# Scores of an attention kernel computed one period earlier, a transpose moved to another PSUM bank, reciprocals moved up in VectorE's order

## Chip, cores and metric

One Trainium2 chip, one of its cores. The metric is the device time of one execution in microseconds (us); lower is better. The engines are TensorE (PE, with its weight loads as PEld), VectorE (DVE), ScalarE (ACT), GpSimd (POOL), and SyncE (SP), which issues the loads and stores here.

## What is computed

Attention that keeps the 32 largest scores of each query, and behind it four chained matrix products on all tokens. Cut to what matters:

```python
B, H, S, D = 8, 8, 576, 64
scores = (1 / 8) * q @ k.T                    # per batch and head, 576 x 576
kth = the 32nd largest score of each row
scores = where(scores >= kth, scores, -1e9)
attn = exp(scores - max) / (sum + 1e-9)
x = (attn @ v) with the heads side by side    # 4608 tokens x 512
out = (((x @ w1) * (x @ w2)) @ w3) @ w_out
```

Inputs and output are float32.

## The kernel before

**Slots and periods.** The queries of a batch are cut into four tiles of 128 and one of 64. A slot is one such tile for one pair of heads (the tiles of 64 take two pairs), so there are 18 slots per batch and 144 in all. A slot has 128 x 2 rows of scores of 576 columns each, in planes `a` = 0 and 1. The loop `for p in range(-1, n_slots + 4)` (line 523) is one period per pass; in it five slots are at different steps: in period `p`, slot `i = p + 1` gets its scores, slot `p` its 32 largest, slot `j = p - 1` its mask and exponentials, slot `l = p - 2` its normalisation, and slot `m = p - 3` its transposition and value products. `InOrder` (line 49) keeps each engine's instructions in the order in which the program records them, so the order of the lines in the loop is the order on each engine, and each engine waits at an instruction until that one may run.

**One period, engine by engine.**
- TensorE: some products of the chained matrices (`fill`), the transposition `turn` (line 291), more `fill`, `scores` (line 201), the value products `values` (line 309), more `fill`. Value products of two slots are put together in every second period (`put_back`), so the time repeats in pairs of periods. Each pair has 48 products of `fill`.
- VectorE: the fold of slot `p`, four operations on two tensors that spread the three thirds of each row into maxima and minima (`w`, in `top32_steps`, line 226); after a period with value products the low halves of `x` (`split_low`); then three rounds of MAX8 and MATCH_REPLACE8 and a last MAX8 on the whole row. Between the rounds it takes the reciprocals of the sums (`invert`) and the product `asb` for the chained matrices.
- ScalarE: two relus that begin the mask (`mask`), the copy of the transposes `tp` back over `pab` and of the odd chunk `pr` (`take_turned`, line 302), two normalisations, the exponentials of plane 0, the copy of the first half of the scores (`take_scores`), the exponentials of plane 1, the second copy of scores, and casts and copies for `x`, `g`, `asb`, `osb`.
- POOL: 1e-9 onto the sums (`add_up`), the thresholds `edge` and the check values `over` from the 32 largest, two masks `pab<-s,pab` of 128 x 576, which are tied behind the fold, and the low halves `g<-asb,g`.

**PSUM.** Eight banks: two buffers of two banks for scores and transposes (`ps_a`; `st` and `tp` take turns in them), one bank `vo`, three for the chained products. A score tile uses columns 0 to 287 of each of its two banks. The transposition of a slot is nine blocks of 128 x 128; eight of them fill `tp`, and the ninth, the odd chunk (columns 512 to 639 of the flat row), is written to `vo[:, :128]`. The value products lie in `vo[:, 256:512]`, where ScalarE (`split_high`) and VectorE (`split_low`) read them.

**The three stretches.** In the first 13 periods the weights are unpacked (`warm`, `decode`), then come the periods with `fill`, and at the end the last block of chained products without attention.

Of the kernel before, what the change touches and what calls it, by code (L numbers as in the profile page):

```python
# [9 lines left out]
F32 = mybir.dt.float32  # L10
# [59 lines left out]
def attn_moe(ctx: ExitStack, tc: tile.TileContext, q, k, v, w1, w2, w3, w_out, out, flag, any_missed, general):  # L70
# [148 lines left out]
    def new_s():  # L219
        return att_p.tile([128, 2, S], F32, tag="s", name="s", bufs=S_BUFS)  # L220

    def take_scores(s, st, h):
        lo, hi = HALVES[h]
        act.copy(s[:, :, lo:hi], st[h][:, :, :HS])

    def top32_steps(s, slot):
        w = att_p.tile([128, 2, S], F32, tag="w", name="w", bufs=1)
        top = tops[slot % len(tops)]
        one, two, three = slice(0, NG), slice(NG, 2 * NG), slice(2 * NG, S)
        dve.tensor_tensor(w[:, :, three], s[:, :, one], s[:, :, two], op=ALU.max)  # L230
        dve.tensor_tensor(w[:, :, two], s[:, :, one], s[:, :, two], op=ALU.min)
        dve.tensor_tensor(w[:, :, one], w[:, :, three], s[:, :, three], op=ALU.max)
        yield dve.tensor_tensor(w[:, :, three], w[:, :, three], s[:, :, three], op=ALU.min)
        for i in range(4):
            cut = slice(i * 8, (i + 1) * 8)
            for a in range(2):
                dve.max(top[:, a, cut], w[:, a, one] if i < 3 else w[:, a, :])
            if i < 3:
                for a in range(2):
                    dve.match_replace(w[:, a, one], top[:, a, cut], w[:, a, one], NEG)  # L240
                yield
# [40 lines left out]
    def invert(sums):  # L282
        dve.reciprocal(sums, sums)
# [4 lines left out]

    vo = ps_v.tile([128, 512], F32, name="vo")

    def turn(pab):
        tp = ps_a.tile([128, 2, 512], F32, tag="a", name="tp")
        flat = pab[:].rearrange("p a c -> p (a c)")
        for a in range(2):
            for c in range(4):
                o = a * (S + 64) + c * 128
                pe.transpose(tp[:, a, c * 128 : (c + 1) * 128], flat[:, o : o + 128], ident)
            if a == 0:
                pe.transpose(vo[:, :128], flat[:, 512:640], ident)
        return tp  # L300

    def take_turned(pab, tp):
        pts = pab[:].rearrange("p a c -> p (a c)")[:, :1024].rearrange("p (a c) -> p a c", a=2)
        act.copy(pts, tp)
        pr = att_p.tile([128, 128], F32, tag="pr", name="pr")
        act.copy(pr, vo[:, :128])
        return pts, pr

    def values(vts, hps, pts, pr, second=False):
# [77 lines left out]
    if general:  # L387
        outs = out.rearrange("e (b t) -> b e t", b=B)
        for src, step in startup:
            for _ in step(fetch(src)):  # L390
                pass
        settle()
        with tc.For_i(0, B, 1) as b:
            seen = small.tile([1, 1], I32, tag="seen", name="seen", bufs=1)
            nc.sync.dma_start(seen, flag[ds(b + 1, 1), :])
            with tc.If(nc.values_load(seen, min_val=0, max_val=1) > 0):
                kts = {hp: load_k(b, hp) for hp in range(NHP)}
                vts = {hp: load_v(b, hp) for hp in range(NHP)}
                for first, ts in ((0, range(3)), (NB, range(3, TAIL + 1))):
                    xs, lo = [new_x(0) for _ in range(NHP)], 0  # L400
                    for t in ts:
                        qt = load_q(b, t)
                        for hps in [hps for hps, u in slots_of(0) if u == t]:
                            s, st = new_s(), scores(qt, kts, hps)
                            for h in range(2):
                                take_scores(s, st, h)
                            edge = top32_exact(s)
                            pab, sums = new_weights()
                            for a in range(2):
                                mask(s, edge, pab, a)  # L410
                                exps(edge, pab, sums, a)
                            add_up(sums)
                            invert(sums)
                            normalise(pab, sums)
                            pts, pr = take_turned(pab, turn(pab))
                            ov = values(vts, hps, pts, pr)
                            for part in parts_of([xs[hp] for hp in hps], lo, t, ov):
                                split_high(*part)
                                split_low(*part)
                        lo += width(t)  # L420
                    place = lambda es: outs[ds(b, 1)][:, es, first : first + lo].rearrange("o p n -> (o p) n")
                    for _ in moe_steps(xs, lo, [(place, slice(0, lo))], lambda f: f()):
                        pass
        return
# [22 lines left out]
        places.append([(lambda es, o=o, w_=w_: out[es, o : o + w_], slice(lo, lo + w_)) for o, lo, w_ in pieces])  # L447
    last_use = {(b, hp): i for i, (b, hps, t) in enumerate(slots) for hp in hps}

    kts, vts, qts, ss, edges, pabs, xs = {}, {}, {}, {}, {}, {}, {}  # L450
    queue, put_off, starting, fresh = [], [], [], []

    def evict():
# [20 lines left out]
    def of(table, b):  # L474
        return {hp: table[b, hp] for hp in range(NHP) if (b, hp) in table}
# [21 lines left out]
    def warm():  # L497
        entered.append(p)
        if p < 0:
            return  # L500
        if fetched and len(entered) % 2 == 0:
            z, step = fetched.pop(0)
            going.append(step(z))
        going[:] = [unit for unit in going if next(unit, "end") != "end"]
        prefetch(WAITING)
# [14 lines left out]
    def share_of(m):  # L520
        return SHARES[m % 2] if put_back(m) or put_back(m - 1) else SHARE

    for p in range(-1, n_slots + 4):
        i, j, l, m = p + 1, p - 1, p - 2, p - 3
        if p == 1:
            vts[0, 0] = load_v(0, 0)
            vts[0, 1] = load_v(0, 1)
            vts[0, 2] = load_v(0, 2)
            vts[0, 3] = load_v(0, 3)
        finder = top32_steps(ss[p], p) if 0 <= p < n_slots else iter(())  # L530
        if 0 <= l < n_slots:
            add_up(pabs[l][1])
        folded = next(finder, None)
        for part in fresh:
            split_low(*part)
        fresh.clear()
        warm()
        if 0 <= j < n_slots:
            edges[j] = edges_of(j)
            pabs[j] = new_weights()  # L540
            for a in range(2):
                mask(ss[j], edges[j], pabs[j][0], a, folded if a == 0 else None)
        warm()
        fill(share_of(m)[0])
        begin()
        next(finder, None)
        if 0 <= m < n_slots:
            turned[m] = take_turned(pabs[m][0], turn(pabs[m][0]))
        if 0 <= l < n_slots:
            invert(pabs[l][1])  # L550
            normalise(*pabs[l])
        if 0 <= j < n_slots:
            exps(edges[j], *pabs[j], 0)
        warm()
        if p == 3:
            stir(6)
        fill(share_of(m)[1])
        next(finder, None)
        warm()
        if i < n_slots:  # L560
            b, hps, t = slots[i]
            st = scores(qts[group_of[i]], of(kts, b), hps)
            ss[i] = new_s()
            take_scores(ss[i], st, 0)
        if 0 <= j < n_slots:
            exps(edges[j], *pabs[j], 1)
        if i < n_slots:
            take_scores(ss[i], st, 1)
            renew(kts, load_k, i)
            if i + 1 == n_slots or group_of[i + 1] != group_of[i]:  # L570
                renew_q(group_of[i] + 2)
        if 0 <= m < n_slots:
            if not put_back(m):
                for n in [m - 1, m] if put_back(m - 1) else [m]:
                    b, hps, t = slots[n]
                    ovs[n] = values(of(vts, b), hps, *turned.pop(n), n < m)
                    renew(vts, load_v, n)
        if p == 14:
            stir(9)
        next(finder, None)  # L580
        warm()
        fill(share_of(m)[2])
        for _ in finder:
            pass
        for d in sorted(ovs):
            b, hps, t = slots[d]
            n = d // BLOCK
            for hp in hps:
                if (n, hp) not in xs:
                    xs[n, hp] = new_x(n)  # L590
            fresh += parts_of([xs[n, hp] for hp in hps], column[group_of[d]], t, ovs.pop(d))
            del ss[d], pabs[d], edges[d]
            if (d + 1) % BLOCK == 0:
                starting.append(n)
        for part in fresh:
            split_high(*part)
        if p == 2:
            stir(8)
        warm()
# [68 lines left out]
```

## Time and profile before

| | |
|---|---|
| median of 3 runs | 1353.26 us (1352.75 to 1353.70) |
| profiled execution | 1352.64 us, span 1350.9 us |
| TensorE busy | 1218.7 us, 90% of the span |
| VectorE busy | 1137.8 us, 84% |
| ScalarE busy | 1116.5 us, 83% |
| POOL busy | 663.1 us, 49% |
| granted TensorE clock, mean | 0.983 |

Times count from the start of the span. An engine's busy time is the union of its instructions; TensorE's products overlap, and their ends are modelled. In a row of waits the first name is the engine and tile that waited, the second the one whose result ended the wait. In a row of a timeline the number in square brackets is the idle time of that engine just before.

### The profile page before, as it was taken

Reading aid. Unit: us, or ns where it says so; the run is one execution under the profiler, and the core shown is the slowest. Engines: PE = TensorE matmul, PEld = TensorE weight load, DVE = VectorE, ACT = ScalarE, POOL = GpSimd, SP = SyncE. Lnnn points to the kernel's source line nnn. Section 1 sums busy time; section 2 is a strip of 40 time slices with the busy share of each in tenths; the row PEclk is TensorE's granted clock in tenths of the full one; section 3 lists DMA queues with packets and bytes.
Section 4 is the critical chain, followed back from the end, with each engine's and each line's share of the span. In section 5 each row is a group of like instructions: output and inputs, shape, how many; then the busy total and the mean of one; then the engine's idle time right before and its main releaser. Section 6 shows DMA issues by size and latency. Waiting matters only on the chain.

```text
span 1350.9 us, 27537 instructions
## 1 busy us (share of the span) xinstructions
PE 1218.7 (90%) x9427; PEld 1034.6 (77%) x9427; DVE 1137.8 (84%) x3952; ACT 1116.5 (83%) x2233; POOL 663.1 (49%) x877
## 2 busy tenths in 40 slices
PE   4888689999999999999999999999999999999998
PEld 3544368888888888888888888888888888888898
DVE  7888999989889889989889889889888889889610
ACT  5888888888888888888888888888888888888821
POOL 4777755445445445445445445445445445445411
PEclk7899889999999999999999999999999999999999
DMA  7334311100120020100120021100120020100000
GB/s 276 111 123 134 102 43 34 42 30 29 33 70 9 15 70 29 42 27 29 34 70 9 14 73 30 37 27 28 35 69 9 15 72 31 37 27 1 7 18 25
DMA packets 30118, 64.73 MB, mean 48 GB/s; under 512 B 5397, under 2 KB 11541, under 8 KB 29973
## 3 DMA queue, kind: packets, MB, share of 16 engines
q1 hardware_dynamic: 29972, 62.93, 14.4%
q8 instruction: 75, 1.23, 0.4%
q14 instruction: 71, 0.57, 0.1%
HBM read 53.48 MB, written 9.44 MB: 47 GB/s over the span
## 4 chain that ended last, share of the span: by engine, by line
ACT 50%; DVE 29%; issue 10%; PE 9%; POOL 2%; ACTq 0%; DVEq 0%; POOLq 0%
ACT pab L59 31%; DVE w L59 19%; ACT s L59 10%; DVE top L59 5%; ACT g L59 3%; PE ab L59 3%; DVE x L59 2%; PE eo L59 2%; PE tp L59 2%; PE vo L59 2%; ACT pr L59 1%; ACT osb L59 1%; ACT asb L59 1%; ACT x L59 1%; POOL edge L59 1%
## 5 line engine op out<-in xcount | busy, mean ns | idle before, releaser
L59 POOL TENSOR_TENSOR pab<-s,pab 128x576 f32<-128x576 f32 x288 | 403.0, 1420 | 286.6 <-DVE w L59 253.7
L59 DVE MAX8 top<-w 128x8 f32<-128x192 f32 (+1 forms) x1152 | 468.5, 450 | 0.0
L59 PE MATMUL ab<-x,wh 128*128 128x384 f32 x1536 | 414.8, 346 | 0.0
L59 DVE MATCH_REPLACE8 w<-top,w 128x192 f32<-128x192 f32 x864 | 290.8, 346 | 0.0
L59 PEld LDWEIGHTS ab<-x,wh 128*128 128x128 f32 x1536 | 274.7, 188 | 6.8 <-issue 6.2
L59 PE MATMUL ab<-x,wl 128*128 128x384 f32 x768 | 264.5, 344 | 0.0
L59 DVE TENSOR_TENSOR w<-s 128x384 f32<-128x384 f32 x288 | 151.3, 564 | 121.9 <-ACT s L59 121.8
L59 ACT COPY pab<-tp 128x1024 f32<-128x1024 f32 x144 | 146.1, 1014 | 114.1 <-PE tp L59 114.1
L59 ACT ACTIVATE pab<-pab,sums 128x576 f32<-128x576 f32 x288 | 208.4, 775 | 33.0 <-DVE sums L59 33.0
L59 ACT ACTIVATE pab<-s,edge 128x576 f32<-128x576 f32 x288 | 209.4, 781 | 27.5 <-POOL edge L59 22.3
L59 PE MATMUL eo<-g,wf 128*128 128x384 f32 x1152 | 226.1, 346 | 0.6 <-POOL g L59 0.5
L59 ACT ACTIVATE pab<-pab,edge 128x576 f32<-128x576 f32 x288 | 223.3, 775 | 1.2 <-POOL pab L59 1.2
L59 PEld LDWEIGHTS eo<-g,wf 128*128 128x128 f32 x1152 | 198.6, 188 | 12.8 <-issue 11.5
L59 PE MATMUL st<-kt,qt 64*128 64x288 f32 (+1 forms) x1280 | 186.2, 437 | 19.8 <-ACT pab L59 6.7
L59 ACT COPY s<-st 128x576 f32<-128x576 f32 x288 | 182.6, 634 | 7.8 <-PE st L59 7.8
L59 POOL TENSOR_TENSOR g<-asb,g 128x384 fp32r<-128x384 f32 x96 | 97.3, 1014 | 181.7 <-ACT g L59 181.7
L59 PE MATMUL tp<-ident,pab 128*128 128x128 f32 x1152 | 170.9, 275 | 6.8 <-ACT s L59 6.8
L59 DVE TENSOR_TENSOR w<-w,s 128x384 f32<-128x384 f32 x288 | 159.3, 553 | 4.9
L59 PE MATMUL vo<-pab,vt 128*64 128x128 f32 (+1 forms) x2560 | 159.1, 268 | 0.0
L59 PEld LDWEIGHTS ab<-x,wl 128*128 128x128 f32 x768 | 144.3, 188 | 17.4 <-issue 17.4
L59 PEld LDWEIGHTS st<-kt,qt 64*128 64x128 f32 (+1 forms) x1280 | 97.3, 179 | 78.1 <-ACT pr L59 30.9
L59 PEld LDWEIGHTS vo<-pab,vt 128*64 128x64 f32 x2560 | 132.2, 139 | 31.3 <-issue 23.5
(50 smaller groups left out, 1137.9 us busy)
## 6 DMA issues: line engine op xcount, KB each, us to landing
z<-in_w SPq DMA_DIRECT2D x32, 512.0 KB, 3.6
vt<-in_v SPq DMA_DIRECT2D x32, 352.0 KB, 4.3
qt<-in_q SPq DMA_DIRECT2D x40, 256.0 KB, 2.7
kt<-in_k SPq DMA_DIRECT2D x32, 320.0 KB, 3.0
out_t<-osb SPq DMA_DIRECT2D x32, 192.0 KB, 1.9
z<-in_wo SPq DMA_DIRECT2D x8, 512.0 KB, 7.5
out_t<-osb SPq DMA_DIRECT2D x16, 160.0 KB, 1.8
out_t<-osb SPq DMA_DIRECT2D x16, 32.0 KB, 1.6
```

Of the source, the lines that this page charges most:

```text
L59: ins = fn(*args, **kw)
```

## The change

The scores are computed for slot `h = p + 2`, one period earlier than before, and kept in `sts` until the next period. Their two copies to SBUF, which stood between the exponentials, are now recorded at the very start of the period, ahead of the relus. The loads of k and q that renew their buffers move with the scores. The loop begins one period earlier. The odd chunk's transpose goes to columns 384 to 511 of the first bank of the second score tile of slot `i` (free columns there) and is copied to `pr` from it; the first bank is read for scores just before. In the last periods, where there is no such tile, a fresh buffer is taken. The reciprocals move from behind the first round of MAX8 to behind the fold (and behind the low halves of `x`).

```diff
@@ -288,22 +288,25 @@
 
     vo = ps_v.tile([128, 512], F32, name="vo")
 
-    def turn(pab):
+    def turn(pab, beside):
         tp = ps_a.tile([128, 2, 512], F32, tag="a", name="tp")
+        if beside is None:
+            beside = ps_a.tile([128, 2, 512], F32, tag="a", name="beside")
+        te = beside[:, 0, 384:]
         flat = pab[:].rearrange("p a c -> p (a c)")
         for a in range(2):
             for c in range(4):
                 o = a * (S + 64) + c * 128
                 pe.transpose(tp[:, a, c * 128 : (c + 1) * 128], flat[:, o : o + 128], ident)
             if a == 0:
-                pe.transpose(vo[:, :128], flat[:, 512:640], ident)
-        return tp
-
-    def take_turned(pab, tp):
+                pe.transpose(te, flat[:, 512:640], ident)
+        return tp, te
+
+    def take_turned(pab, tp, te):
         pts = pab[:].rearrange("p a c -> p (a c)")[:, :1024].rearrange("p (a c) -> p a c", a=2)
         act.copy(pts, tp)
         pr = att_p.tile([128, 128], F32, tag="pr", name="pr")
-        act.copy(pr, vo[:, :128])
+        act.copy(pr, te)
         return pts, pr
 
     def values(vts, hps, pts, pr, second=False):
@@ -412,7 +415,7 @@
                             add_up(sums)
                             invert(sums)
                             normalise(pab, sums)
-                            pts, pr = take_turned(pab, turn(pab))
+                            pts, pr = take_turned(pab, *turn(pab, st[1]))
                             ov = values(vts, hps, pts, pr)
                             for part in parts_of([xs[hp] for hp in hps], lo, t, ov):
                                 split_high(*part)
@@ -447,7 +450,7 @@
         places.append([(lambda es, o=o, w_=w_: out[es, o : o + w_], slice(lo, lo + w_)) for o, lo, w_ in pieces])
     last_use = {(b, hp): i for i, (b, hps, t) in enumerate(slots) for hp in hps}
 
-    kts, vts, qts, ss, edges, pabs, xs = {}, {}, {}, {}, {}, {}, {}
+    kts, vts, qts, sts, ss, edges, pabs, xs = {}, {}, {}, {}, {}, {}, {}, {}
     queue, put_off, starting, fresh = [], [], [], []
 
     def evict():
@@ -520,20 +523,26 @@
     def share_of(m):
         return SHARES[m % 2] if put_back(m) or put_back(m - 1) else SHARE
 
-    for p in range(-1, n_slots + 4):
-        i, j, l, m = p + 1, p - 1, p - 2, p - 3
+    for p in range(-2, n_slots + 4):
+        h, i, j, l, m = p + 2, p + 1, p - 1, p - 2, p - 3
         if p == 1:
             vts[0, 0] = load_v(0, 0)
             vts[0, 1] = load_v(0, 1)
             vts[0, 2] = load_v(0, 2)
             vts[0, 3] = load_v(0, 3)
         finder = top32_steps(ss[p], p) if 0 <= p < n_slots else iter(())
+        if 0 <= i < n_slots:
+            ss[i] = new_s()
+            take_scores(ss[i], sts[i], 0)
+            take_scores(ss[i], sts[i], 1)
         if 0 <= l < n_slots:
             add_up(pabs[l][1])
         folded = next(finder, None)
         for part in fresh:
             split_low(*part)
         fresh.clear()
+        if 0 <= l < n_slots:
+            invert(pabs[l][1])
         warm()
         if 0 <= j < n_slots:
             edges[j] = edges_of(j)
@@ -545,9 +554,8 @@
         begin()
         next(finder, None)
         if 0 <= m < n_slots:
-            turned[m] = take_turned(pabs[m][0], turn(pabs[m][0]))
+            turned[m] = take_turned(pabs[m][0], *turn(pabs[m][0], sts[i][1] if i < n_slots else None))
         if 0 <= l < n_slots:
-            invert(pabs[l][1])
             normalise(*pabs[l])
         if 0 <= j < n_slots:
             exps(edges[j], *pabs[j], 0)
@@ -557,18 +565,14 @@
         fill(share_of(m)[1])
         next(finder, None)
         warm()
-        if i < n_slots:
-            b, hps, t = slots[i]
-            st = scores(qts[group_of[i]], of(kts, b), hps)
-            ss[i] = new_s()
-            take_scores(ss[i], st, 0)
+        if h < n_slots:
+            b, hps, t = slots[h]
+            sts[h] = scores(qts[group_of[h]], of(kts, b), hps)
+            renew(kts, load_k, h)
+            if h + 1 == n_slots or group_of[h + 1] != group_of[h]:
+                renew_q(group_of[h] + 2)
         if 0 <= j < n_slots:
             exps(edges[j], *pabs[j], 1)
-        if i < n_slots:
-            take_scores(ss[i], st, 1)
-            renew(kts, load_k, i)
-            if i + 1 == n_slots or group_of[i + 1] != group_of[i]:
-                renew_q(group_of[i] + 2)
         if 0 <= m < n_slots:
             if not put_back(m):
                 for n in [m - 1, m] if put_back(m - 1) else [m]:
@@ -589,7 +593,7 @@
                 if (n, hp) not in xs:
                     xs[n, hp] = new_x(n)
             fresh += parts_of([xs[n, hp] for hp in hps], column[group_of[d]], t, ovs.pop(d))
-            del ss[d], pabs[d], edges[d]
+            del ss[d], pabs[d], edges[d], sts[d]
             if (d + 1) % BLOCK == 0:
                 starting.append(n)
         for part in fresh:
```

On ScalarE, in a pair of steady periods with products `ab`, before. `s<-st` are the copies of scores, `pab<-s,edge` the relus, `pab<-tp` and `pr<-vo` the copies of the transposes, `pab<-pab,sums` the normalisations, `pab,sums<-pab,edge` the exponentials:

```order
L59 CAST g<-asb 128x384
L59 COPY s<-st 128x2x288
L59 ACTIVATE pab,sums<-pab,edge 128x576
L59 COPY s<-st 128x2x288
L59 ACTIVATE pab<-s,edge 128x576 x2
L59 COPY asb<-ab 128x384
L59 COPY pab<-tp 128x1024
L59 COPY pr<-vo 128x128
L59 ACTIVATE pab<-pab,sums 128x576 x2
L59 ACTIVATE pab,sums<-pab,edge 128x576
```

The same place with the change:

```order
L59 CAST g<-asb 128x384
L59 ACTIVATE pab,sums<-pab,edge 128x576
L59 COPY s<-st 128x2x288 x2
L59 ACTIVATE pab<-s,edge 128x576 x2
L59 COPY asb<-ab 128x384
L59 COPY pab<-tp 128x1024
L59 COPY pr<-st 128x128
L59 ACTIVATE pab<-pab,sums 128x576 x2
L59 ACTIVATE pab,sums<-pab,edge 128x576
```

The first score copy has moved from ahead of the second exponentials to behind them, so both stand together ahead of the relus; they are those of the next slot but one that VectorE folds, no longer of the next. The odd chunk is copied from `st`.

On VectorE, in one steady period whose predecessor had value products, before (`x<-vo,x` are the low halves):

```order
L59 TENSOR_TENSOR w<-s 128x2x192 x2
L59 TENSOR_TENSOR w<-w,s 128x2x192 x2
L59 TENSOR_TENSOR x<-vo,x 128x128 x2
L59 MAX top_100<-w 128x8 x2
L59 MATCH_REPLACE w<-top_100,w 128x192 x2
L59 RECIPROCAL sums<-sums 128x2
L59 TENSOR_TENSOR asb<-ab,asb 128x384
```

The same place with the change:

```order
L59 TENSOR_TENSOR w<-s 128x2x192 x2
L59 TENSOR_TENSOR w<-w,s 128x2x192 x2
L59 TENSOR_TENSOR x<-vo,x 128x128 x2
L59 RECIPROCAL sums<-sums 128x2
L59 MAX top_100<-w 128x8 x2
L59 MATCH_REPLACE w<-top_100,w 128x192 x2
L59 TENSOR_TENSOR asb<-ab,asb 128x384
```

The reciprocals stand ahead of the first round instead of behind it. On TensorE the steady order of a period is as before, with `st` in place of `vo` as the target of the odd chunk's transpose.

## Rows read from the trace of the kernel before

**Rows 1.** Windows: length, busy PE, PEld, DVE, ACT, POOL, granted clock, DMA share, GB/s

```profile
200.00:1250.00 1050.00, 980.26 (x8048) 858.28 (x8047) 934.21 (x3336) 913.09 (x1848) 503.83 (x709) 1.00 0.11 35
701.15:718.02 16.87, 15.77 (x124) 13.82 (x124) 15.30 (x55) 14.90 (x30) 8.74 (x14) 1.00 0.00 1
1300.00:1351.00 51.00, 46.42 (x264) 46.02 (x262) 4.67 (x10) 9.38 (x19) 8.09 (x8) 1.00 0.05 17
```

**Rows 2.** Waits of the whole span: us in total, times, longest

```profile
PE vo L59 <- DVE x L59: 83.1, 68, 4.7
```

**Rows 3.** Waits from 200 to 1250 us, the same columns

```profile
POOL g L59 <- ACT g L59: 134.0, 85, 2.4
DVE w L59 <- ACT s L59: 111.5, 125, 1.5
...
PE vo L59 <- DVE x L59: 69.7, 62, 1.4
```

**Rows 4.** Timeline of TensorE: start, length, instruction, count, idle time before and its end

```profile
701.70 0.60 PE L59 MATMUL tp<-ident,pab 128*128 128x128 f32 x4
702.13 0.27 PE L59 MATMUL vo<-ident,pab 128*128 128x128 f32 x1
...
709.92 0.60 PE L59 MATMUL tp<-ident,pab 128*128 128x128 f32 x4
711.62 0.33 PE L59 MATMUL vo<-ident,pab 128*128 128x128 f32 x1 [1.10 <-DVE x L59]
...
719.07 0.60 PE L59 MATMUL tp<-ident,pab 128*128 128x128 f32 x4
```

**Rows 5.** Timeline of ScalarE, the same pair

```profile
709.60 1.47 ACT L59 ACTIVATE pab<-s,edge 128x576 f32<-128x576 f32 x2
712.47 1.02 ACT L59 COPY pab<-tp 128x1024 f32<-128x1024 f32 x1 [1.41 <-PE tp L59]
...
717.35 0.64 ACT L59 COPY s<-st 128x576 f32<-128x576 f32 x1
718.06 1.44 ACT L59 ACTIVATE pab<-s,edge 128x576 f32<-128x576 f32 x2
...
719.77 1.01 ACT L59 COPY pab<-tp 128x1024 f32<-128x1024 f32 x1
```

**Rows 6.** Timeline of VectorE, the same pair

```profile
701.15 1.03 DVE L59 TENSOR_TENSOR w<-s 128x384 f32<-128x384 f32 x2 [1.51 <-ACT s L59]
...
715.51 1.42 DVE L59 MAX8 top<-w 128x8 f32<-128x576 f32 x2
718.02 1.04 DVE L59 TENSOR_TENSOR w<-s 128x384 f32<-128x384 f32 x2 [1.08 <-ACT s L59]
```

**Rows 7.** Timeline of POOL, the same pair

```profile
711.33 2.80 POOL L59 TENSOR_TENSOR pab<-s,pab 128x576 f32<-128x576 f32 x2 [2.11 <-DVE w L59]
716.23 1.02 POOL L59 TENSOR_TENSOR g<-asb,g 128x384 fp32r<-128x384 f32 x1 [2.10 <-ACT g L59]
717.54 0.21 POOL L59 TENSOR_SCALAR sums<-sums 128x2 f32<-128x2 f32 x1 [0.29 <-ACT pab L59]
717.83 0.20 POOL L59 TENSOR_TENSOR edge<-top,coef 128x4 f32<-128x4 f32 x1
```

**Rows 8.** Timelines of VectorE and POOL in the start, where folds meet POOL's operations

```profile
89.39 1.57 POOL L59 TENSOR_TENSOR edge<-top,coef 128x4 f32<-128x4 f32 x1
...
153.38 2.38 DVE L59 TENSOR_TENSOR w<-s 128x384 f32<-128x384 f32 x2
153.76 1.59 POOL L59 TENSOR_TENSOR z<-z 128x512 int32<-128x512 int32 x1
...
177.56 1.26 POOL L59 TENSOR_TENSOR wl<-z,wh 128x512 fp32r<-128x512 f32 x1 [1.19 <-ACT wh L59]
178.90 0.41 POOL L59 TENSOR_SCALAR sums<-sums 128x2 f32<-128x2 f32 x1
179.39 0.37 POOL L59 TENSOR_TENSOR edge<-top,coef 128x4 f32<-128x4 f32 x1
```

## The prediction

> **What bounds the kernel now.** I read the windows view first, because the run has three stretches: a start in which weights are decoded, a long steady stretch, and a tail without attention. From 200 to 1250 us [rows 1] TensorE is busy for 980.26 of 1050 us (93%), VectorE for 934.21 (89%) and ScalarE for 913.09 (87%). No engine has much room, so a saving on one is worth only what the next one leaves.
>
> Then the waits. TensorE's one large wait is for VectorE's work on x: 83.1 us in 68 waits [rows 2], 69.7 us in 62 waits in the steady stretch [rows 3], 1.12 us each. It comes once in two periods. VectorE's own large wait there is for the score copies, 111.5 us in 125 waits [rows 3], 0.89 us each. A period is the work on one slot; I count in pairs of periods, since the value products of two slots are done together in the second one.
>
> Then the timelines of one pair, from fold to fold 701.15 to 718.02, 16.87 us [rows 6], with TensorE busy for 15.77, VectorE 15.30 and ScalarE 14.90 us [rows 1]. TensorE issues the four first transposes at 709.92, and the odd chunk's transpose, which in the undisturbed period follows 0.43 us later (701.70 to 702.13), comes only at 711.62 [rows 4]. It writes columns 0 to 127 of the bank whose columns 256 to 511 VectorE is still reading for the low halves of x. VectorE reaches those reads late, because they stand behind the fold, and the fold waits for the second score copy (1.51 and 1.08 us in the two folds shown, [rows 6]). ScalarE then waits 1.41 us for the transposes [rows 5]. So the pair is a loop over three engines with one avoidable wait on each.
>
> **The change part by part.**
>
> *The odd chunk's transpose into the scores' bank.* It removes the wait at 711.62: 1.10 us by the idle time of that row, 711.62 - (709.92 + 0.43) = 1.27 us by the starts [rows 4]. It adds a condition: the transpose may not start until the second score copy of this period has left the bank. In the new order of ScalarE that copy ends two copies after the x casts, and the relus follow it; in the old timeline the relus start at 709.60 [rows 5], and the two score copies and the casts end before them. The transpose would want to go at 710.35. So I cost the new condition at nothing; its cover is 0.75 us, and beyond that it stalls TensorE one for one.
>
> The Trainium skill, PSUM — Partial Sum Buffer, section "PSUM bank collisions raise a hardware error", says that accesses have to be kept apart by bank and not by column; the wait of this trace over disjoint columns agrees with it. By that rule the transpose still has a bank to wait for, only another one; whether it costs is the last rival's matter.
>
> *Score copies first in the period.* The same two copies move from between the exponentials to ahead of the next relus. ScalarE does the same work between one copy of the transposes and the next: 712.47 to 719.77 in the old order, 7.30 us, with no wait marked [rows 5]; TensorE ends the transposes concerned at 719.07 + 0.60 = 719.67 [rows 4], so ScalarE is 0.10 us behind. In the other period the relus end at 709.60 + 1.47 = 711.07, and without the stall the copy of the transposes could start at 712.47 - 1.27 = 711.20, so ScalarE is 0.13 us ahead. The order as such costs nothing, but ScalarE has almost no slack against an unstalled TensorE.
>
> *The fold no longer waits.* Scores are a period old when the fold wants them, so the 0.89 us wait goes. VectorE's floor is its 15.30 us per pair. That is below TensorE's, so this part by itself is not on the path; what it does is start the fold where POOL is still at work. In the old timeline the last MAX8 starts at 715.51 and the one row shown for two lasts 1.42, so a fold without a wait starts at about 716.9; POOL's subtraction for g holds 716.23 to 717.25, and the sums and edge operations follow [rows 6, 7]. Before, these three ran in the fold's wait and cost nothing.
>
> What they cost in each other's way is seen where the start of the run lets them meet [rows 8]: two fold operations took 2.38 us instead of 1.03 while a POOL operation on two tensors was running, so VectorE stood still for what was left of it; the small POOL operations took 0.41 and 0.37 us instead of 0.20, and in the worst row 1.57 us. After a long POOL operation that ended at 177.56 + 1.26 = 178.82, the edges were done at 179.76, and the relus that want them can start 0.03 us later (717.83 + 0.20 to 718.06, [rows 5, 7]): 0.97 us. Undisturbed it is 718.06 - 717.54 = 0.52 us.
>
> The Trainium skill, SBUF — State Buffer, section "SBUF: two separate sides", speaks against this part: it says that VectorE operations with two SBUF inputs and POOL operations exclude each other for a whole instruction, and whichever starts first holds the other up. The 2.38 us agree. By that rule alone each subtraction may cost VectorE up to its whole 1.02 us, and the forecast would be 1343 us instead of 1284, by the rows' own account of it in the second rival below.
>
> Placed by hand, as an estimate: VectorE runs ahead until the fold lands behind the subtraction. In the period that the old timeline shows, the relus are ready for ScalarE's sake when the second score copy is through, by 717.35 + 0.64 = 717.99 at the latest, and the edges allow them at 717.25 + 0.97 = 718.22. That is 0.23 us late, and since ScalarE has no slack in that period I pass all of it, 0.25, to TensorE; in the other one, with the x casts between, it is covered. VectorE's pair is then 15.30 plus about 0.4 us of standing still, 15.7, still under TensorE's.
>
> *Reciprocals behind the fold.* They are ready earlier for the normalisations; ScalarE waits for the transposes anyway in each pair [rows 5], so I count nothing. It adds a wait: the reciprocal needs the sums operation on POOL, which needs the last exponential of the period before, and behind it on VectorE stand all rounds of MAX8. The exponentials end about when the new fold starts, and the fold's two pairs of operations take some 2 us (1.03 for the first pair, [rows 6]), so it is hidden; if the sums operation takes 1.57 us it still is.
>
> *Loads.* SP issues the q and k loads a period (8.4 us) earlier, each after the last scores that use the buffer. They are hidden before and after; the pair shown has a DMA share of 0.00 [rows 1].
>
> **The sum.** A pair without the stall is 15.77 us by TensorE's busy time, or 16.87 - 1.27 = 15.60 by the starts. With 0.25 us for late relus where subtractions fall (85 of them to 62 pairs, [rows 3], so about 1.4 per pair) it is 15.8 us. That is 1.07 us less per pair. Of the 68 waits 65 lie in such pairs, the other three in the start, where they hold 83.1 - 65 x 1.12 = 10 us. There VectorE and ScalarE set the pace with the decoding, and I take nothing, with 0 to 10 us gained as bounds. The tail is TensorE at 46.42 of 51 us [rows 1] with the same products, and stays. 65 x 1.07 = 69.6 us. The profiled execution took 1352.64 us, 0.6 under the median of the three runs, 1353.26; against the median the forecast is 1284 us.
>
> **The rivals.** A difference of 0.2%, 2.7 us, is about what a measurement of this kernel can tell from none.
>
> *All of it and more*: the relus are never late, pairs take 15.6 us and the start gains too: 65 x 1.27 + 10 = 93 us, 1261. For it: VectorE has 0.3 us to find a better place. Against: three engines within 1 us of each other. Chance 0.08.
>
> *The port takes it*: each subtraction meets a fold. VectorE then needs 15.30 + 1.4 x 1.02 = 16.7 us per pair and sets the pace: 65 x 0.15 = 10 us gained, 1343. If only half of them do, 16.0 us and about 1297 us. For it: the subtraction overlaps the undelayed fold already in the old timeline. Against: VectorE that is held up starts its next fold later, so that it falls behind the subtraction by itself. I give 0.25 to everything between 1300 and 1350.
>
> *It slides further, and the kernel is slower*: POOL's two masks (2.80 us together, [rows 7]) follow the relus. If the relus start more than about 4 us after the fold (one relu, half of 1.44, [rows 5], and a little before the first mask, 2.80 for both, of VectorE's period of 15.30 / 2 = 7.65), the second mask reaches into the next fold and holds VectorE up there as well, which makes the next edges and relus later again. With half a mask, 0.7 us, in both periods on top of the subtractions a pair is 16.7 + 1.4 = 18.1 us, 65 x 1.2 = 80 us more, 1433 us. For it: ScalarE has no slack. Against: by my placing the relus start 1.0 to 1.5 us after the fold. Chance 0.09.
>
> *The wait only changes its name*: the transpose now waits for the score copy, which ScalarE makes later in the pair than I placed it, and TensorE loses the same 1.1 us: 1353 us. For it: the bank has still another reader. Against: 0.75 us of cover. Chance 0.06.
>
> **How the numbers follow.** The forecast case, 1272 to 1300 us, has 0.52. The likeliest is 1284. The range 1264 to 1332 takes in most of the first rival and over half of the second, and leaves out some 0.2. Faster: 0.52 + 0.08 + 0.25 = 0.85; same 0.06; slower 0.09.
>
> **What would show it.** Right: no wait of TensorE for x; no wait of VectorE for the score copies; steady pairs of 15.6 to 15.9 us between first folds of alternate slots; edge operations of 0.4 us and more instead of 0.20; some folds lengthened by a subtraction, under 0.5 us per pair in all; ScalarE's wait for the transposes mostly gone. Wrong: pairs of fold operations that take 1.6 us and more instead of 1.03 in most periods, a new wait of TensorE for ScalarE's copies of scores or transposes above 0.3 us per period, or a start that grows.

## The result and the profile after

The changed kernel takes 1267.72 us (median of 4 runs, 1266.17 to 1267.84) where the kernel before takes 1353.01 (4 runs): a ratio of 0.937, 95% interval 0.935 to 0.938. 85 us are gone. The forecast was 1284 with a range of 1264 to 1332.

The windows view of the kernel before, with the columns of [rows 1]:

```profile
200.00:1160.00 960.00, 895.78 (x7340) 784.09 (x7338) 854.23 (x3050) 834.74 (x1687) 460.27 (x648) 1.00 0.12 37
```

The same stretch, and the last 51 us, of the changed kernel:

```profile
200.00:1160.00 960.00, 959.92 (x7974) 853.44 (x7972) 936.57 (x3314) 903.53 (x1832) 581.10 (x703) 1.00 0.12 37
1213.30:1264.30 51.00, 46.43 (x264) 46.02 (x262) 4.67 (x10) 9.38 (x19) 8.09 (x8) 1.00 0.05 17
```

By the profile, which models the ends of its products, TensorE has no idle time left in the steady stretch: it is busy for 959.92 of 960 us, before the change for 895.78. The last stretch is the same as in [rows 1] (46.43 against 46.42 us busy). The chain that ended last, as shares of the span by engine, before:

```profile
ACT 50%; DVE 29%; issue 10%; PE 9%; POOL 2%; ACTq 0%; DVEq 0%; POOLq 0%
```

and after:

```profile
PE 85%; ACT 7%; POOL 3%; DVE 2%; issue 1%; DMA 1%; SPq 0%; POOLq 0%; ACTq 0%
```

Before, it ran along ScalarE and VectorE; now it runs along TensorE.

The length of a pair is read from the first fold operation of slots 24 and 132 (counted from 0), 54 pairs apart, on VectorE's timeline, before:

```profile
263.08 1.03 DVE L59 TENSOR_TENSOR w<-s 128x384 f32<-128x384 f32 x2 [1.08 <-ACT s L59]
...
1173.98 1.04 DVE L59 TENSOR_TENSOR w<-s 128x384 f32<-128x384 f32 x2 [1.08 <-ACT s L59]
```

and after:

```profile
256.95 1.07 DVE L59 TENSOR_TENSOR w<-s 128x384 f32<-128x384 f32 x2
...
1095.21 1.09 DVE L59 TENSOR_TENSOR w<-s 128x384 f32<-128x384 f32 x2
```

That is 910.90 / 54 = 16.87 us before and 838.26 / 54 = 15.52 us after: 1.345 us less per pair, where the forecast had 1.07.

The waits from 200 to 1160 us, before (us in total, times, longest):

```profile
PEld vo L59 <- DVE x L59: 77.7, 57, 1.7
PE vo L59 <- DVE x L59: 64.2, 57, 1.4
```

and after:

```profile
POOL g L59 <- ACT g L59: 151.0, 84, 2.0
...
ACT pab L59 <- PE tp L59: 34.0, 72, 0.5
...
PEld st L59 <- ACT pr L59: 23.0, 92, 0.3
...
ACT pab L59 <- POOL edge L59: 10.0, 42, 0.2
```

TensorE's wait for x and VectorE's wait for score copies [rows 3] have no row there any more. The wait of TensorE for x was all of TensorE's idle time before (960 - 895.78 = 64.2). Of the three engines with little room it is ScalarE that waits now: for the transposes (0.47 us each) and for the edges (0.24 us each). TensorE's weight loads wait 23.0 us for the small copy `pr`, while its products go on.

Now the places where the prediction had expected trouble. TensorE, with the transposes of a period behind x casts:

```profile
670.21 0.60 PE L59 MATMUL tp<-ident,pab 128*128 128x128 f32 x4
670.64 0.27 PE L59 MATMUL st<-ident,pab 128*128 128x128 f32 x1
```

VectorE in the same period:

```profile
667.41 1.45 DVE L59 TENSOR_TENSOR w<-s 128x384 f32<-128x384 f32 x2
668.78 1.14 DVE L59 TENSOR_TENSOR w<-w,s 128x384 f32<-128x384 f32 x2
669.84 0.48 DVE L59 TENSOR_TENSOR x<-vo,x 128x128 fp32r<-128x128 f32 x2
```

POOL:

```profile
666.97 1.01 POOL L59 TENSOR_TENSOR g<-asb,g 128x384 fp32r<-128x384 f32 x1 [2.00 <-ACT g L59]
668.06 0.40 POOL L59 TENSOR_SCALAR sums<-sums 128x2 f32<-128x2 f32 x1
668.54 0.38 POOL L59 TENSOR_TENSOR edge<-top,coef 128x4 f32<-128x4 f32 x1
668.87 0.51 POOL L59 TENSOR_TENSOR over<-top 128x2 f32<-128x2 f32 x1
```

ScalarE:

```profile
668.42 1.20 ACT L59 COPY s<-st 128x576 f32<-128x576 f32 x2
669.48 1.48 ACT L59 ACTIVATE pab<-s,edge 128x576 f32<-128x576 f32 x2
671.44 1.01 ACT L59 COPY pab<-tp 128x1024 f32<-128x1024 f32 x1 [0.49 <-PE tp L59]
```

VectorE's low halves of x end at 669.84 + 0.48 = 670.32, ahead of the odd chunk's transpose at 670.64. The fold meets the subtraction for g, and its first two operations take 1.45 instead of 1.03 us. The edges are done at 668.92; but the relus stand behind the two score copies and start at 669.48 in any case. ScalarE then still waits 0.49 us for the transposes.

### The profile page after: what moved, and what is told of

Read it like the earlier page. It is cut to its first block, busy times and chain, and to the rows that moved or that the text cites. A ratio compares the mean times of both kernels' runs of the same rounds, so it can differ in the third digit from the quotient of the medians.

```text
span 1264.3 us, 27411 instructions
## 1 busy us (share of the span) xinstructions
PE 1202.5 (95%) x9427; PEld 1037.2 (82%) x9427; DVE 1145.3 (91%) x3952; ACT 1112.5 (88%) x2233; POOL 748.1 (59%) x877
## 4 chain that ended last, share of the span: by engine, by line
PE 85%; ACT 7%; POOL 3%; DVE 2%; issue 1%; DMA 1%; SPq 0%; POOLq 0%; ACTq 0%
PE ab L59 33%; PE eo L59 16%; PE st L59 13%; PE vo L59 12%; PE tp L59 9%; ACT pab L59 4%; ACT z L59 1%; POOL z L59 1%; POOL edge L59 1%; DMA kt<-in_k 1%; DVE w L59 1%; PE pf L59 1%; DVE top L59 0%; DVE z L59 0%; DVE t L59 0%
## 5 line engine op out<-in xcount | busy, mean ns | idle before, releaser
L59 ACT COPY s<-st 128x576 f32<-128x576 f32 x288 | 171.0, 654 | 10.4 <-PE st L59 10.4
L59 DVE TENSOR_TENSOR w<-s 128x384 f32<-128x384 f32 x288 | 156.6, 584 | 17.3 <-ACT s L59 7.0
L59 PEld LDWEIGHTS tp<-ident,pab 128*128 128x128 f32 x1152 | 141.3, 142 | 19.7 <-ACT s L59 10.3
```

The source lines that it names most:

```text
L59: ins = fn(*args, **kw)
```

## The experiments

Three parts can be done alone: T, the transpose's new bank; R, the reciprocals moved up; S, scores a period ahead and copied first. The edits of the diff stand ahead of the prediction, so a part is named by its lines.

**T alone.** The kernel before, with the odd chunk in columns 384 to 511 of a second score tile (that of slot `p`, since no later one is there yet):

```diff
-                pe.transpose(vo[:, :128], flat[:, 512:640], ident)
+                pe.transpose(te, flat[:, 512:640], ident)
...
-        act.copy(pr, vo[:, :128])
+        act.copy(pr, te)
```

> The kernel before with the odd chunk's transpose alone moved, into the scores' bank. Theory A (the transpose's bank is what paid): TensorE's wait for x is gone, pairs of about 15.7 us, 1275 to 1290 us in all, although VectorE still waits for score copies. Theory B (the fold that waited for the copies is what paid): the pair stays bound by the chain of copies, fold and reciprocal, above 16.2 us, 1310 us or more.

Measured: 1310.91 us, ratio 0.969 (0.968 to 0.971). Only half of the gain. The wait for x is gone, yet TensorE is idle for 960 - 928.63 = 31 us of the steady stretch. VectorE's and ScalarE's timelines of this kernel say why. VectorE:

```profile
705.50 1.04 DVE L59 TENSOR_TENSOR w<-s 128x384 f32<-128x384 f32 x2 [0.43 <-ACT s L59]
...
709.09 0.15 DVE L59 RECIPROCAL sums<-sums 128x2 f32<-128x2 f32 x1
...
713.81 1.04 DVE L59 TENSOR_TENSOR w<-s 128x384 f32<-128x384 f32 x2 [0.43 <-ACT s L59]
...
717.01 0.15 DVE L59 RECIPROCAL sums<-sums 128x2 f32<-128x2 f32 x1
```

ScalarE:

```profile
709.34 1.45 ACT L59 ACTIVATE pab<-pab,sums 128x576 f32<-128x576 f32 x2 [0.76 <-DVE sums L59]
...
713.15 0.62 ACT L59 COPY s<-st 128x576 f32<-128x576 f32 x1
...
717.25 1.44 ACT L59 ACTIVATE pab<-pab,sums 128x576 f32<-128x576 f32 x2 [0.51 <-DVE sums L59]
```

Its waits, 200 to 1160 us:

```profile
ACT pab L59 <- DVE sums L59: 84.5, 118, 1.1
DVE w L59 <- ACT s L59: 68.2, 119, 0.9
```

There is a second loop, through VectorE and ScalarE alone: fold, first round, reciprocal (709.09), normalisations (709.34, ScalarE waited 0.76 us for them), exponentials, second score copy (ends 713.77), next fold (713.81). It takes 8.31 us where the low halves of x stand in it and, by the folds, 7.91 where they don't: 16.22 us per pair. Before, by the folds, the two periods of a pair took 8.97 us with x and 7.90 without it (means of the 54 pairs): T shortens only the first. Both engines wait for each other in every period (118 and 119 times), and neither is ever busy throughout.

**R alone.** The kernel before, with the reciprocals behind the fold:

```diff
+        if 0 <= l < n_slots:
+            invert(pabs[l][1])
         warm()
...
-            invert(pabs[l][1])
             normalise(*pabs[l])
```

> The kernel before with the reciprocals alone moved ahead of the first round. Loop theory (the kernel before runs at a loop fold, first round, reciprocal, normalisations, exponentials, score copies, next fold, 7.9 us per period): the loop loses the first round, 1.17 us, so the fold and with it x come earlier, the wait for x falls below 0.3 us, 1270 to 1300 us. Rival (a reciprocal costs what its 0.16 us and its wait on ScalarE say, 0.5 us in every second period, hidden by the wait for the transposes): 1335 to 1353 us.

Measured: 1324.51 us, ratio 0.979 (0.977 to 0.980). A miss: it lies between the range expected and that of its rival. The second loop is open: periods without x take 7.48 us instead of 7.90, and ScalarE has no wait for sums. But the wait for x stays, and periods with it take 8.95 us, against 8.97 before. So R shortens just the period that T leaves as it was: both loops held the kernel before, one in each period of a pair. TensorE:

```profile
714.35 0.60 PE L59 MATMUL tp<-ident,pab 128*128 128x128 f32 x4
715.75 0.33 PE L59 MATMUL vo<-ident,pab 128*128 128x128 f32 x1 [0.80 <-DVE x L59]
```

VectorE releases it at 715.21 + 0.48 = 715.69, when the low halves of x end:

```profile
715.21 0.48 DVE L59 TENSOR_TENSOR x<-vo,x 128x128 fp32r<-128x128 f32 x2
```

Pairs take 16.44 us. The reciprocals, which the prediction counted at nothing, are worth 29 us here.

**T and R, scores as before.**

> Transpose and reciprocals moved, scores where they were. Loop theory: no loop over the score copies is longer than TensorE's 15.5 us per pair any more, 1268 to 1285 us, although the fold still follows the score copies of its own slot. Rival: the copies between the exponentials hold the fold up on their own, 1295 us or more.

Measured: 1275.42 us, ratio 0.943 (0.941 to 0.944), pairs of 15.68 us. Both loops are open without moving a score, and 8 us are left. VectorE still waits for score copies, 33.0 us in 76 waits from 200 to 1160 us, and TensorE is busy for 952 of 960 us; that the one is the reason for the other is not shown.

**S alone, and the change without T or without R.** S is the rest of the diff that stands ahead of the prediction; T and R are the two blocks above, left out or undone:

```diff
+            take_scores(ss[i], sts[i], 0)
+            take_scores(ss[i], sts[i], 1)
...
+            sts[h] = scores(qts[group_of[h]], of(kts, b), hps)
```

> Only the scores and their copies moved; transpose and reciprocals as in the kernel before. Theory B: within 10 us of the run with the transpose put back, below 1295 us. Theory A: 1335 us or more. If both parts are needed, between 1295 and 1335 us.

> The changed kernel with the odd chunk's transpose put back into the bank of the value products. Theory A: the wait for x comes back, some 1.1 us per pair, 1335 us or more. Theory B: with a fold that waits for nothing, VectorE is through with x before TensorE wants that bank (in the changed kernel's trace 0.3 us before), so 1268 to 1285 us.

> The changed kernel with the reciprocals put back behind the first round of MAX8. As forecast, they count nothing: 1266 to 1271 us. Rival: ScalarE has no slack in the changed kernel, so a reciprocal that comes 1.1 us later stops the normalisations as before (0.5 us in every second period) and TensorE with them: 1285 to 1300 us.

Measured: S alone 1269.00 us, ratio 0.938 (0.937 to 0.940); the change without T 1268.74 (0.937 to 0.940); without R 1266.88 (0.935 to 0.938). None can be told from the change itself (0.935 to 0.938). TensorE is busy for 959.9 to 960.0 of 960 us in all three, and none has a wait for x in the steady stretch, also where the odd chunk is in `vo` still. In the run of S alone, VectorE ends the low halves of x at 672.57 + 0.48 = 673.05:

```profile
672.57 0.48 DVE L59 TENSOR_TENSOR x<-vo,x 128x128 fp32r<-128x128 f32 x2
```

TensorE's transpose into their bank starts 0.33 us later, without a wait:

```profile
673.38 0.27 PE L59 MATMUL vo<-ident,pab 128*128 128x128 f32 x1
```

So S gives all of the gain, and on top of it T and R give nothing that can be measured.

**Shares.** Which stall is left? The chained products of a period are dealt out otherwise, two of them moved from behind the value products to between the transposes and the scores:

```diff
-SHARE = 8, 8, 8
-SHARES = (8,8,12), (8,8,4)
+SHARE = 8, 10, 6
+SHARES = (8,10,10), (8,10,2)
```

> The changed kernel with two chained products more per period between transposes and scores, and two fewer at its end (8, 10, 6 instead of 8, 8, 8; 10 and 10, 10 and 2 in the pairs). If TensorE's 960 of 960 us are only modelled ends over a wait of 0.25 us per period for the copy of the odd chunk, that wait goes and pairs fall to VectorE's 15.2 us: 1245 to 1260 us. If TensorE has no time left at all: 1265 to 1270 us.

Measured: 1264.58 us, ratio 0.935 (0.933 to 0.937), pairs of 15.50 us. That is 0.4 us under the second range expected, and what a TensorE without idle time leaves: between these two orders of its work there is next to no difference.

**Each subtraction for g done twice.** This puts the price of the second rival on the chip. The operation on POOL is recorded twice in `take_b`:

```diff
             pool.tensor_tensor(gf[:, 1, :nb], whole, gf[:, 0, :nb].bitcast(F32), op=ALU.subtract)
+            pool.tensor_tensor(gf[:, 1, :nb], whole, gf[:, 0, :nb].bitcast(F32), op=ALU.subtract)
```

> The changed kernel with POOL's subtraction for g done twice, the same result written again; 96 operations of 1.01 us more on POOL, which is busy for 59%. If a POOL operation holds the fold up for what is left of it: 0.5 to 1.0 us per period in two thirds of the pairs, of which VectorE's slack of 0.4 us per pair hides a part, so 1285 to 1330 us. If folds and POOL operations only take turns at operation ends as the small ones do: 1265 to 1272 us.

Measured: 1326.49 us, ratio 0.980 (0.978 to 0.982), pairs of 16.39 us: 0.87 more than the change. The groups of the steady stretch (all instructions of one kind together: count, busy us, mean ns) show the first two operations of each fold, in the change:

```profile
L59 DVE TENSOR_TENSOR w<-s 128x384 f32<-128x384 f32 x248 | 135.6, 587 | 10.0
```

and here:

```profile
L59 DVE TENSOR_TENSOR w<-s 128x384 f32<-128x384 f32 x234 | 181.0, 813 | 9.4
```

At four operations to a pair, the fold's busy time goes from 135.6 / 62 = 2.19 to 181.0 / 58.5 = 3.09 us per pair, 0.91 more, close to the 0.87 by which the pair grew; VectorE is now busy for 939.83 of 960 us and TensorE for 914.46. One place, on POOL:

```profile
702.79 2.11 POOL L59 TENSOR_TENSOR g<-asb,g 128x384 fp32r<-128x384 f32 x2 [1.42 <-ACT g L59]
```

VectorE, whose first fold operation begins inside it:

```profile
704.12 1.20 DVE L59 TENSOR_TENSOR w<-s 128x384 f32<-128x384 f32 x1
```

and ScalarE, whose relus have become late:

```profile
705.88 1.45 ACT L59 ACTIVATE pab<-s,edge 128x576 f32<-128x576 f32 x2 [1.33 <-POOL edge L59]
```

POOL's two subtractions end at 704.90, and the fold operation, 1.20 us long where it takes 0.56 on its own, at 705.32. The mechanism of the second rival is real; it needs a POOL that works further into the fold than it does in the change.

**Fewer chained products.** What bounds after TensorE? One of the three products of each piece is left out, with two thirds of the shares:

```diff
-                    for n, (w, x) in enumerate(((wh, 0), (wh, 1), (wl, 0))):
+                    for n, (w, x) in enumerate(((wh, 0), (wh, 1))):
...
-                for n, (i, j) in enumerate(((0, 0), (1, 0), (0, 1))):
+                for n, (i, j) in enumerate(((0, 0), (1, 0))):
```

> Leaves out one of the three products of every piece of the four chained matrices (wl x and wf g-low), so each pair of periods has 32 such products instead of 48 and the shares of a period are two thirds; all else is the change. If TensorE is the only bound left in the change (busy 959.9 of 960 us there), pairs fall from 15.52 us to whatever bounds next: VectorE's own work is 936.6 of 960 us, 15.14 us per pair, ScalarE's 14.6, so 15.1 to 15.3 us, with VectorE busy for over 97% and TensorE below 90%; 65 x 0.3 = 20 us, and the last stretch without attention loses a third of its 46 us of products, 15 us: 1226 to 1240 us. If instead a loop over engines (relus late, copies late) holds the change at nearly the same pace beside TensorE, pairs stay at 15.4 to 15.5 us with no engine at 97%, and only the last stretch shortens: 1245 to 1253 us.

Measured: 1225.89 us, at the lower end of the range expected, pairs of 15.23 us. Its windows view:

```profile
200.00:1160.00 960.00, 847.36 (x7108) 690.03 (x7100) 945.57 (x3375) 910.74 (x1865) 592.71 (x716) 0.99 0.12 37
```

VectorE is busy for 98.5% of the stretch and TensorE for 88%. So with fewer products VectorE is the bound, and the pair is only 0.29 us shorter than with TensorE as the bound. The stretch behind the last fold shrank from 83.9 to 62.9 us, more than the 15 expected.

**The second keys earlier.** In the changed kernel the first two folds are 14.6 us apart (7.02 and 21.61), before it 9.8. TensorE's timeline of the change:

```profile
11.99 4.09 PE L59 MATMUL st<-kt,qt 64*128 64x288 f32 x16 [5.75 <-DMA kt<-in_k]
```

Slot 1's scores, now a period earlier, wait for keys whose load stands behind four weight loads on SP; on ScalarE their copies stand ahead of the decoding of the weights. The edit:

```diff
-    prefetch(4)
     kts[0, 1] = load_k(0, 1)
+    prefetch(4)
```

> The change, with the load of the second pair of heads' keys issued ahead of the four weight loads instead of behind them. In the change the second slot's scores waited 5.75 us for that load, and the second fold came 14.6 us after the first (9.8 before the change). Theory: the delay of the start is that load; the second fold comes 3 to 6 us earlier. Since the change had made up for its late second fold by the 16th slot (194.6 us against 195.4 before), the decoding of the weights sets that pace and little of it should reach the end: 1263 to 1268 us. Rival: the start is a chain from slot to slot and all of it reaches the end: 1261 to 1264 us. If the weight loads that now land later hold the decoding up: 1268 to 1272 us.

Measured: 1261.69 us, ratio 0.933 (0.931 to 0.934). VectorE's timeline of this kernel:

```profile
7.61 1.03 DVE L59 TENSOR_TENSOR w<-s 128x384 f32<-128x384 f32 x2 [7.61 <-ACT s L59]
...
17.43 1.02 DVE L59 TENSOR_TENSOR w<-s 128x384 f32<-128x384 f32 x2
```

The second fold is 4.2 us earlier than in the change, and the last one still 4.4 us (1175.95 against 1180.34). The theory that the decoding sets the pace falls; the rival holds, the start is a chain from slot to slot. That slot 16 of the change is level with that of before (its first fold at 194.66 against 195.35) came from two effects that hid each other: a late second fold, and about as much gained by shorter periods behind it.

**Both.** The shares and the early keys together, as the version to beat both kernels.

> The change with both the other shares of chained products (10 between the transposes and the scores, 6 behind; 1264.6 us by itself against 1267.7) and the early load of keys. If the two do not touch each other, the sum of what each gives alone: 1258 to 1265 us, pairs of 15.50 us and TensorE without idle time in the steady stretch. Rival: nothing beyond the shares, 1264 to 1266 us.

Measured: 1260.97 us (5 runs, 1260.11 to 1261.42), ratio 0.932 (0.931 to 0.933). It beats the change (0.935 to 0.938), but can't be told from the early keys alone; the shares bring at most a little.

## Why the prediction was right, and where its reasons were not

*The sign and the bound.* Right: TensorE becomes the bound, its wait for x goes, VectorE's wait for scores goes. 1267.7 lies in the range, between the first rival (1261) and the forecast case (from 1272).

*"The transpose's new bank removes the wait."* This is the step that failed, though the sum came near. By itself T removes that wait and gives 42 us, because the second loop takes over at 16.22 us per pair. S removes the wait without T: its fold starts earlier, so that VectorE is through with x before TensorE wants the bank (673.05 against 673.38 in the run of S alone). The prediction saw that the fold made VectorE late, but credited the wait to the bank that was named in its row. That the sum came near is luck as far as this step goes: it took a pair to be TensorE's own work, and that is what is left whichever part removes the stall. The last rival's wait, of the transposes for score copies, has no row in the steady stretch of the change.

*"By itself not on the path", of the fold.* Wrong. VectorE's floor of 15.30 us is its busy time, and the prediction compared that floor alone with TensorE. The loop over the fold, the reciprocals and the score copies, 16.22 us in the run of T alone, is longer than either engine's work (15.30 and 14.90 us in [rows 1]). It could be read from before: VectorE waited for score copies 125 times, so in every period, not once in two as TensorE did [rows 3], and the chain that ended last was ScalarE's and VectorE's for 79% of the span. The prediction didn't read the chain.

*"I count nothing" for the reciprocals.* Right for the change, where S has cut the loop already (R undone: no difference). Wrong as a price of the part: alone it is worth 29 us, with T 35 us more than T alone.

*1.27 us per stall, 1.07 per pair.* Under-priced. The pair became 1.345 us shorter. The row of TensorE's products gave 64.2 / 57 = 1.13 us, that of its weight loads 77.7 / 57 = 1.36, and the latter is nearer: around the stall, products that count as busy take longer too (895.78 us busy in 56.9 pairs are 15.74 us a pair before, and 15.52 after, for the same products). The sum itself is loose: 0.25 on top of 15.60 or of 15.77 us gives 15.85 or 16.02, and its 15.8 fits only the former; by the latter the forecast would have been about 1298. The measured 15.52 lies below both starting values.

*0.25 us for late relus.* Nothing of it reached TensorE. The small POOL operations did grow as the row of the start showed, here in the group of the change and then of before (busy us, mean ns):

```profile
L59 POOL TENSOR_TENSOR edge<-top,coef 128x4 f32<-128x4 f32 x124 | 45.5, 367 | 9.9
```

```profile
L59 POOL TENSOR_TENSOR edge<-top,coef 128x4 f32<-128x4 f32 x114 | 22.5, 198 | 9.2 <-POOL sums L59 0.2
```

But the relus stand behind two score copies of 1.20 us, which cover it, and ScalarE waits 0.47 us for the transposes afterwards. That ScalarE has no slack was read from one pair of the old timeline; in the new order it is busy for 903.53 of 960 us.

*VectorE's 0.4 us of standing still.* 0.10 us: the fold's first operations take 2.19 us per pair against 118.8 / 57 = 2.08 in the group of before, 228 operations. The second rival's meeting did come, and its price did not: by the single operations of the trace, each of the 84 subtractions from 200 to 1160 us has a fold beginning inside it, but on average only 0.21 us before its end, and the fold's first operation takes 0.66 us there against 0.56 elsewhere. So the fold does not fall behind the subtraction, as the prediction has it, but into its last part; what keeps it there is not shown. Where more than 0.15 us of the subtraction were left, 52 times, that operation ended 0.41 or 0.42 us after the subtraction. By the Trainium skill (SBUF — State Buffer, section "SBUF: two separate sides") the engine that comes second is held up to the end of the other's instruction. The folds of 1.45 us and the doubled subtraction agree with it. The 2.38 us of [rows 8] hold two such waits, the first of them for a POOL operation that ended at 153.80 and is not shown there.

*The start.* Nothing was taken for it, and nothing came (0.7 us by slot 16), but not for the reason given: 4 to 6 us lay in the order of the loads on SP, where the scores, now a period earlier, find their keys behind the weights. For the loads the prediction looked at the steady stretch alone.

The sum, with the sizes measured: 1070.71 us lie between the folds of slot 16 and of the last slot before (195.35 to 1266.06) and 985.68 after (194.66 to 1180.34), 85.0 us less; 0.7 come from the start and 0.9 from what follows the last fold.

## What to carry to other kernels

A wait in the profile names the last thing that was late, not the loop that made it late: before crediting a change, follow the waiting engine's order back to its own start, and list each closed loop over the engines with its length. Where two engines wait for each other in every period, that loop is a bound, even if neither is busy all the time. When work is moved a period ahead, look at the first period too: what it needs may stand far back in a load queue.

## What the runs showed of the hardware

The small POOL operations that arrive during a fold of the changed kernel do not wait for the end of the fold, but for the end of one of its operations: `sums`, `edge` and `over` took 0.40, 0.38 and 0.51 us at 668.06 to 669.38, in the midst of four fold operations that ran from 667.41 to 669.92. They ended 0.06 to 0.07 us after the first, the second and the third of these (668.39, 668.86 and 669.33). It isn't always the next one: the `edge` of 1.57 us in [rows 8] ended 0.06 us after the third fold operation that ran beside it. A longer POOL operation in the same place (666.97 to 667.98) held the fold of 667.41 up by 0.42 us, most of what was left of it, and the doubled one by 0.64. So in these rows what the two engines cost each other goes by the length of the instruction that is already running, and short ones cost the other little.
